# Moving two pairs of DMA transposes behind the x loads, and two spectrum loads two steps up, in a fused FFT-filter and mixer kernel

## The chip, the core and the metric

The kernel runs on one core of a Trainium2 chip. The time is the device time in microseconds (us) of one execution. The core has five engines that work side by side: PE (TensorE, matrix products), DVE (VectorE), ACT (ScalarE), POOL (GpSimd) and SP (SyncE). In this kernel DVE and ACT empty PE's result banks and do the elementwise work, SP issues most DMAs (transfers within the core's memory, between it and DRAM, and DMA transposes), and POOL issues the loads of x and the stores of the output. An engine works through its instructions in order: an instruction that waits holds back all that stand behind it on that engine.

## The reference

Two stages follow each other. The first is a global filter along the sequence, the second a low-rank mixing along the sequence with a two-layer channel network:

```python
batch, seq, dim = 8, 3136, 256          # rank 32, hidden 1024
X = np.fft.rfft(x, axis=1)
Y = X * (filt_r + 1j * filt_i)[None]
x = np.fft.irfft(Y, n=seq, axis=1)

h = x.transpose(0, 2, 1) @ U @ V        # mixes the sequence through rank 32
u = x + h.transpose(0, 2, 1)
out = u + np.maximum(u @ w_ch1, 0.0) @ w_ch2
```

Inputs and output are float32; the kernel computes in float16 with float32 sums.

## The kernel before, in words

The transform of length 3136 is split as 49 x 64. For each batch the kernel does these stages, in the code's names:

- `load_x`: four tiles of x per batch (called c = 0 to 3 here), issued by POOL, each 98 partitions by 2048 numbers, converted from float32 to float16 on the way. The tag has four buffers.
- `f1`: the 49-point transforms on PE (line 249), emptied by ACT (line 254). After every fourth step the result goes to DRAM (`ct1`, and `ct0` for the lowest frequency), issued by SP (lines 256 and 257). Sixteen steps per batch, four for each tile of x.
- `mid`: first the loads of `a2` from `ct1` and `ct0` (lines 327 and 330, SP). Then, for twelve pairs of frequencies and the lowest one, a product (`pz`, lines 384 and 386), the filter on DVE (line 392, then 396 and 397), and three steps later the way back (`pe`, line 344), which ACT copies to `e3` (line 354). Every second pair is written to DRAM by SP (line 362) in `ct2[b][0]`, `ct2[b][1]` or `ct2[b][2]`, two writes to each.
- `load_e2`: the three thirds of `ct2` come back as rows of `eb` (line 415), two DMAs of 256 KB for each third, issued by SP. `eb` has one buffer. The changed line names these thirds p = 0, 1, 2.
- `rank`: the low-rank part, on PE, ACT and DVE (DVE copies rows into `eb`, line 437).
- `s4`: the last transform (`pu`, line 455) from `eb` to `ut`, with the mixed sequence u in `ut`.
- The channel network runs over 49 groups of 512 rows of u. `mm1` (line 487) makes one eighth of the hidden layer, ACT applies the rectifier (line 490). `mm2` (line 520) makes the output of the group before. The summand u is added in one of two ways. For a group in `turning`, `turn_u` brings u turned into the tile `tur` by DMA transposes (line 500, two per piece of a batch, so one pair for most groups), issued by SP, and DVE adds it while it empties the bank (line 533). For the other groups PE adds it (line 512) and DVE only copies (line 536). `tur` has three buffers. POOL stores a group of the output (line 540).

The order is written out by hand. The main loop has 392 steps, eight per group: step 8n + t does `mm1` of group n and `mm2` of group n - 1 for part t, and then whatever `plan[8n + t]` holds. The loop `for b in range(1, NB)` fills the plan: while the channel network works on batch b - 1 (steps a to z, with a, z = `S[b-1]`, `S[b]`), the stages of batch b and the `f1` of batch b + 1 are dealt over the steps. `deal(gen, count, a, z)` puts `count` steps of a stage evenly between two steps. `e` marks the end of `mid`: e = 76, 124, 172, 220, 266, 314 for b = 2 to 7. For b = 2, a = 48 and z = 96.

The plan sets an order for each engine, not a time. An SP instruction runs as soon as those before it in SP's queue have been issued and what it reads, or the buffer it writes, is ready.

What stands in the plan around the change, for b = 2: `turn_u` of groups 7, 8 and 9 at steps 49, 50, 51; the four loads of x of batch 3 at steps 48 to 51; `ct2` writes at 53 and 57 (first third), 61 and 67 (second), 72 and 74 (last); `f1` of batch 3 from step 58 on, with its writes at 61, 65, 70 and 74; the loads of `eb` at 71, 72 and 77; the first step of `mid` of batch 3 (its `a2` loads) at 78; `s4` from step 85 on. For the later batches the same stands at the same distances from e, but for small shifts.

Of the kernel before, what the change touches and what calls it, by code (L numbers as in the profile page):

```python
# [79 lines left out]
def kernel(  # L80
# [465 lines left out]
    def deal(gen, count, a, z):  # L546
        for i in range(count):
            plan[max(0, int(a + i * (z - a) / count))].append(gen)

    def later_x(b, c):  # L550
        load_x(b, c)
        yield

    def turn_at(at, n):
        turning.add(n)
        plan[at].append(turns[n])
# [55 lines left out]
    def loads(b, part):  # L612
        load_e2(b, part)
        yield

    for b in range(1, NB):
        a, z = S[b - 1], S[b]
        e = z - (17 if b == 1 else 20 if b < 6 else 22)
        deal(mids[b], 13, a + {1: 8, 2: -3}.get(b, -5), e - 4)
        deal(mids[b], 4, e - 4, e)  # L620
        for p, at in enumerate((e - 5, e - 4, e + 1)):
            plan[at].append(loads(b, p))
        deal(ranks[b], 6, e, e + 6)
        if b + 1 < NB:

            plan[z - 12 if b == 1 else e + 2].append(mids[b + 1])

        n = a // 8 + (1 if b > 1 else 2)
        for i in range(3):
            turn_at(a + (15 if b == 1 else 1) + i, n + i)  # L630
        turn_at(z - (15 if b == 1 else 9), z // 8 - 1)
        deal(s4s[b], 16, e + (8 if b == 1 else 9), z - (2 if b == 1 else 1))
        if b == 1:
            deal(f1s[1], 12, 1, 8)
        if b + 1 < NB:

            for c in range(4):
                plan[a + {1: 9 + 2 * c, 2: c}.get(b, 2 * c - 8)].append(later_x(b + 1, c))
            deal(f1s[b + 1], 16, a + (21 if b == 1 else 10), z - (13 if b == 1 else 20))
# [43 lines left out]
```

## Time and profile before

| What | Value |
|---|---|
| median of the runs shown | 507.56 us (505.39 to 508.66) |
| time of the profiled execution | 509.21 us |
| its span (first to last recorded work) | 507.4 us |
| PE busy | 482.4 us (95%) |
| ACT busy | 375.7 us (74%) |
| DVE busy | 350.2 us (69%) |
| POOL busy | 82.4 us (16%) |
| mean granted PE clock | 0.996 of full speed |
| DMA | 97.26 MB, mean 192 GB/s |

The busy time of an engine is the time in which it works on an instruction; time in which it only waits is not in it. PE's busy time also holds time in which it runs at a lower clock. The time lies 1.8 us above the span: that part is outside the recorded work.

### The profile page before, as it was taken

The page shows a single profiled execution, that of the slowest core. Times are in us where ns is not written, and L with a number is a line of the kernel's source. Part 1 is how long each engine was busy: PE and PEld are TensorE (multiplying, and loading weights), DVE is VectorE, ACT ScalarE, POOL GpSimd, SP SyncE. Part 2 cuts the span into 40 slices and gives each one's busy share as a digit, 9 for nine tenths or more (in the row PEclk, how much of TensorE's full clock was granted, in tenths as well). Part 3 has the DMA queues.
Part 4 walks back from the last instruction along what each step waited for, and adds up shares of the span by engine and source line. Part 5 has one row for each costly group of instructions (what it writes and reads, how often), then busy time and mean ns, then how long its engine had stood idle before and what let it go on. Part 6 is the DMA issues. An engine that isn't in the chain of part 4 may idle for free.

```text
span 507.4 us, 11552 instructions
## 1 busy us (share of the span) xinstructions
PE 482.4 (95%) x4584; PEld 339.1 (67%) x4584; DVE 350.2 (69%) x470; ACT 375.7 (74%) x704; POOL 82.4 (16%) x125
## 2 busy tenths in 40 slices
PE   3788899997999999999999999999999999999997
PEld 3536566775667777677666777677667766776665
DVE  5796599588657897479747897579846995642122
ACT  6875778966796689857995689867996677666663
POOL 6773110012001200120102101021001010101110
PEclk9999999999899999999999999999999999999999
DMA  8998769989967995899678975899789447843343
GB/s 188 178 224 160 122 138 217 283 228 186 202 190 257 194 222 168 267 288 171 196 220 279 180 196 149 267 262 192 208 247 246 129 113 226 129 125 89 99 105 126
DMA packets 105383, 97.26 MB, mean 192 GB/s; under 512 B 42971, under 2 KB 89883, under 8 KB 105328
## 3 DMA queue, kind: packets, MB, share of 16 engines
q1 hardware_dynamic: 90560, 54.87, 46.4%
q0 software_dynamic: 14768, 41.65, 33.6%
q8 instruction: 36, 0.59, 0.5%
q14 instruction: 19, 0.16, 0.1%
HBM read 55.07 MB, written 47.64 MB: 202 GB/s over the span
## 4 chain that ended last, share of the span: by engine, by line
PE 75%; DMA 7%; DVE 5%; issue 4%; ACT 2%; POOL 1%; SPq 0%; POOLq 0%; ACTq 0%
PE pc L520 29%; PE phh L487 28%; PE pf L249 4%; PE pu L455 4%; PE pe L344 4%; PE pz L384 3%; DVE uv L392 3%; DMA x<-in_x_dram 3%; DMA w2sb<-in_moe_w_ch_dram 2%; DMA eb<-ct 2%; PE pc L512 1%; DMA ct<-e 1%; PE ph L422 1%; ACT e L354 1%; DVE uv L396 0%
## 5 line engine op out<-in xcount | busy, mean ns | idle before, releaser
L490 ACT ACTIVATE h<-phh 128x512 f16<-128x512 f32 x392 | 235.9, 604 | 80.7 <-PE phh L487 79.9
L520 PE MATMUL pc<-w2sb,h 128*128 128x256 f16 x1568 | 234.4, 273 | 1.3 <-DMA w2sb<-in_moe_w_ch_dram 0.8
L487 PE MATMUL phh<-ut,w1sb 128*128 128x512 f16 (+7 forms) x896 | 233.7, 353 | 0.5 <-DVE ut L462 0.5
L520 PEld LDWEIGHTS <-h 128*128 128x128 f16 x1568 | 151.9, 98 | 92.6 <-issue 2.4
L392 DVE TENSOR_TENSOR uv<-pz,fab 128x1024 f16<-128x1024 f32 (+1 forms) x104 | 120.4, 1178 | 11.1 <-PE pz L384 9.3
L540 POOL DMA_DIRECT2D out_dram<-och x48 | 38.8, 809 | 391.2 <-DVE och L533 256.8
L533 DVE TENSOR_TENSOR och<-pc,tur 128x512 f32<-128x512 f32 (+1 forms) x71 | 48.4, 682 | 76.7 <-PE pc L520 75.5
L487 PEld LDWEIGHTS <-w1sb 128*128 128x128 f16 x896 | 80.0, 97 | 20.6 <-issue 1.6
L354 ACT CAST e<-pe 128x512 f16<-128x512 f32 x96 | 56.6, 591 | 16.9 <-PE pe L344 16.0
L462 DVE CAST ut<-pu 128x392 f16<-128x392 f32 x92 | 48.3, 560 | 21.6 <-PE pu L455 18.5
L254 ACT CAST asb<-pf 98x512 f16<-98x512 f32 x96 | 57.3, 599 | 3.8 <-PE pf L249 3.5
L437 DVE COPY eb<-h 32x4096 f16<-32x4096 f16 x32 | 38.2, 1231 | 13.7 <-ACT h L434 13.7
L344 PE MATMUL pe<-uv,m 128*128 128x512 f16 (+1 forms) x117 | 41.5, 373 | 2.3 <-DVE uv L392 1.6
L455 PE MATMUL pu<-sv,eb 97*128 97x49 f16 x1024 | 39.1, 185 | 2.1 <-DMA eb<-ct 1.1
L249 PE MATMUL pf<-x,ws 98*98 98x256 f16 x192 | 37.0, 275 | 2.9 <-DMA x<-in_x_dram 2.8
L455 PEld LDWEIGHTS <-eb 97*128 97x128 f16 x1024 | 37.1, 96 | 3.9 <-issue 2.6
L384 PE MATMUL pz<-a,m 128*128 128x512 f16 x96 | 36.4, 381 | 1.1 <-DVE a L310 1.0
L396 DVE TENSOR_TENSOR uv<-uv 64x1024 f16<-64x1024 f16 (+1 forms) x49 | 30.8, 629 | 1.7
L249 PEld LDWEIGHTS <-ws 98*98 98x98 f16 x192 | 23.1, 127 | 12.8 <-issue 4.3
L397 DVE TENSOR_TENSOR uv<-uv 64x1024 f16<-64x1024 f16 (+1 forms) x49 | 30.8, 628 | 0.7
L536 DVE COPY och<-pc 128x512 f32<-128x512 f32 x28 | 19.4, 691 | 15.1 <-PE pc L512 13.8
L460 ACT CAST ut<-pu 128x392 f16<-128x392 f32 x36 | 17.5, 485 | 7.8 <-POOL seen L603 4.6
(80 smaller groups left out, 237.8 us busy)
## 6 DMA issues: line engine op xcount, KB each, us to landing
out_dram<-och POOLq DMA_DIRECT2D x48, 512.0 KB, 4.7
ct<-e SPq DMA_DIRECT2D x47, 256.0 KB
eb<-ct SPq DMA_DIRECT2D x46, 256.0 KB
x<-in_x_dram POOLq DMA_DIRECT2D x28, 392.0 KB, 10.0
ct<-asb SPq DMA_DIRECT2D x24, 384.0 KB
a<-ct SPq DMA_DIRECT2D x18, 512.0 KB
x<-in_x_dram POOLq DMA_DIRECT2D x4, 384.0 KB, 8.7
tur<-ut SPq DMA_TRANSPOSE x70
```

What stands on the lines that cost most here:

```text
L249: nc.tensor.matmul(pf[0:98, 256 * s:256 * s + 256], ws[:, (8 * c + j) * 98:(8 * c + j + 1) * 98], t[:, j, :], start=(s == 0), stop=True, s ...
L254: nc.scalar.copy(dst, src)
L344: nc.tensor.matmul(pe[:, 0:n], w, uv[:, f, o:o + n], start=(f == 0), stop=(b > 0 or f == 1))
L354: nc.scalar.copy(t[:, 2 * (i % 2):2 * (i % 2) + 2, :].rearrange("p k d -> p (k d)"), pe)
L384: nc.tensor.matmul(pz, a2m, src[:, k:k + 2, :].rearrange("p k d -> p (k d)"), start=True, stop=True)
L392: nc.vector.tensor_mul(uv[:, :, o:o + n], zin, fin)
L455: nc.tensor.matmul(pu[:, NQ * i:NQ * i + NQ], eb[:, 8 * n + i, d], sv[:, 8 * g + i, :], start=(i == 0), stop=True, skip_group_check=True)
L462: nc.vector.tensor_copy(dst, src)
L487: nc.tensor.matmul(ph[:, o:o + n], w1sb[:, dh, 128 * t:128 * t + 128], utv(b)[:, dh, t0:t0 + n], start=(dh == 0), stop=(dh == 1), skip_gro ...
L490: nc.scalar.activation(h, ph, RELU)
L520: nc.tensor.matmul(o, gr.h[tt][:, 128 * i:128 * i + 128], w2sb[:, tt, :], start=(tt == 0), stop=(tt == 7 and gr.n in turning), skip_group_ ...
L533: nc.vector.tensor_add(dst.rearrange("p g (h d) -> p g h d", h=2), src.rearrange("p (g h d) -> p g h d", h=2, d=128), gr.tu[:, :, a:a + n, ...
```

## The change

Two places of the loop that fills the plan are edited.

- The loads of `eb` of thirds 0 and 1 stand at steps e - 7 and e - 6 in place of e - 5 and e - 4, for every batch from b = 2 on. Third 2 stays at e + 1.
- For b = 2 alone, `turn_u` of groups 8 and 9 stands at steps 60 and 61 in place of 50 and 51. Group 7 stays at step 49.

No instruction is added or removed.

```diff
         e = z - (17 if b == 1 else 20 if b < 6 else 22)
         deal(mids[b], 13, a + {1: 8, 2: -3}.get(b, -5), e - 4)
         deal(mids[b], 4, e - 4, e)
-        for p, at in enumerate((e - 5, e - 4, e + 1)):
+        for p, at in enumerate((e - 5, e - 4, e + 1) if b == 1 else (e - 7, e - 6, e + 1)):
             plan[at].append(loads(b, p))
...
         n = a // 8 + (1 if b > 1 else 2)
         for i in range(3):
-            turn_at(a + (15 if b == 1 else 1) + i, n + i)
+            turn_at(a + {1: 15 + i, 2: (1, 12, 13)[i]}.get(b, 1 + i), n + i)
```

## The prediction

> **What bounds the kernel now.** I read the page first. PE is busy for nearly the whole span and carries 75% of the chain of work that ended last, so an edit that adds and removes no instruction can only change time in which PE waits, or PE's clock.
>
> ```profile
> PE 482.4 (95%) x4584; PEld 339.1 (67%) x4584; DVE 350.2 (69%) x470; ACT 375.7 (74%) x704; POOL 82.4 (16%) x125
> PE 75%; DMA 7%; DVE 5%; issue 4%; ACT 2%; POOL 1%; SPq 0%; POOLq 0%; ACTq 0%
> ```
>
> Next come the waits of PE, longest first. Asked stretch by stretch, those after the prologue that touch this change are two: the f1 of batch 3 waits for x, and the s4 of batch 4 waits for eb.
>
> ```profile
> PE pf L249 <- DMA x<-in_x_dram: 2.8, 1, 2.8
> PE pu L455 <- DMA eb<-ct: 1.1, 1, 1.1
> ```
>
> The chain in order of time (start, duration, what) shows where. The first wait ends at 127.09, the second at 273.80.
>
> ```profile
> 114.05 13.00 DMA x<-in_x_dram
> 127.05 0.04 issue
> 127.09 0.38 PE pf L249 x2
> ...
> 263.54 5.76 DMA ct<-e
> ...
> 269.35 4.31 DMA eb<-ct
> 273.66 0.14 issue
> 273.80 0.57 PE pu L455 x16
> ```
>
> The table by stretches shows that the first wait costs more than its length. Behind the busy times, the third column from the right is the granted clock: 0.58, 0.50, 0.50, 0.71 in the four microseconds after it.
>
> ```profile
> 128.00:129.00 1.00, 1.00 (x8) 0.69 (x6) 0.36 (x1) 0.60 (x2) 0.00 (x0) 0.58 1.27 214
> 129.00:130.00 1.00, 1.00 (x5) 0.53 (x4) 0.97 (x2) 0.51 (x2) 0.00 (x0) 0.50 1.34 134
> 130.00:131.00 1.00, 1.00 (x5) 0.48 (x4) 0.59 (x1) 0.73 (x3) 0.00 (x0) 0.50 1.19 102
> 131.00:132.00 1.00, 1.00 (x7) 0.79 (x6) 0.00 (x0) 0.53 (x2) 0.00 (x0) 0.71 1.88 87
> ```
>
> PE loses 0.42 + 0.50 + 0.50 + 0.29 = 1.71 us there. So the wait for x costs 2.82 + 1.71 = 4.53 us. After the wait for eb the clock stays at 1.00: that one costs 1.10 us.
>
> **Part 1, the transposes of groups 8 and 9.** SP's timeline has the six transposes of groups 7, 8 and 9 from 110.75 on, while POOL issues x from 114.05.
>
> ```profile
> 110.75 16.54 SPq L500 DMA_TRANSPOSE tur<-ut  x6
> 127.39 6.89 SPq L362 DMA_DIRECT2D ct<-e  x3
> ```
>
> Four transposes (groups 7 and 8) go at once. Group 9 needs the tur buffer of group 5, which DVE releases at 121.82 (an add at 121.14 for 0.68). All ct2 writes behind it stand until 127.39. The packet records say the same: a pair is 1,024 packets of 256 B; group 7's are through by 114, group 8's begin then and trickle at some 50 per us between 120 and 127, beside x packets of 322 ns.
>
> What does x take without them? The first x tile takes 13.0 us to land here and 12.7 in the next batch (issued at 164.80, transposes beside it). In the two batches after (220.80 and 278.29), where the records show the pairs in flight done before x starts, it is 6.5 and 6.1 us. So with group 8 away I expect the tile at 114.05 + 6.1 to 6.5 = 120.2 to 120.6, and PE asks for it at 127.09 - 2.82 = 124.27: a margin of 3.7 us. If nothing but half of the delay went, it would land at 123.8, still in time; the gain is bounded by 0 and 4.53 us, and I take 4.53, by the nearest rows.
>
> The Trainium skill, page "DMA: Bandwidth & Descriptors", section "Queues, rings and completion order", speaks against this: each DMA engine takes turns between its rings, a packet at a time. By that, 31 ns of transpose beside each 322 ns x packet would slow x by a tenth, and x would have been in time already. The 13.0 against 6.1 us does not agree. It is rival B's ground.
>
> What the moved pairs meet: in SP's queue they now stand behind the ct2 writes of steps 53 and 57. The second of those waits for ACT's copy at 123.44 + 0.58 = 124.02, so group 8's pair goes at some 124.5, group 9's after the next ct2 write. They need 1.2 to 2.5 us of SP each. Behind them are ct2 and ct1 writes, which today leave at 127.39 to 134.41 anyway. DVE wants the turned rows at steps 75 and 83, over 15 us later. The second to fourth x tiles, by the rows of 220.80 (8.1, 9.7, 11.8 us), land by 122.7 to 127.6; PE needs them four, eight and twelve steps after 124.27, a step being some 1.3 us, so from 129 on. What is late next is DVE: it lags PE by 1.5 us at 124.4 (a product of 122.90 read at 124.40). The same lag stands at 184.10 in the next batch, where PE waits for nothing. So I put nothing there.
>
> **Part 2, the loads of two thirds of eb.** SP's timeline in batch 3:
>
> ```profile
> 197.53 0.39 SPq L362 DMA_DIRECT2D ct<-e  x1
> 201.61 0.30 SPq L256 DMA_DIRECT2D ct<-asb  x1
> 201.96 0.39 SPq L257 DMA_DIRECT2D ct<-asb  x1
> 202.40 1.23 SPq L415 DMA_DIRECT2D eb<-ct  x2
> 203.73 0.54 SPq L362 DMA_DIRECT2D ct<-e  x1
> 204.37 2.24 SPq L415 DMA_DIRECT2D eb<-ct  x2
> 206.66 0.65 SPq L362 DMA_DIRECT2D ct<-e  x1
> ```
>
> Two steps up, the first third goes right behind the ct2 write of 197.53, the second as soon as that write has landed; both now stand ahead of the ct1 write of 201.61. This adds a wait at the head of SP's queue. The packets of that write end at 199.5, and the DMA engines then idle:
>
> ```profile
> 199.50:201.50 2.00, 2.00 (x16) 1.43 (x15) 1.95 (x3) 1.97 (x5) 0.00 (x0) 1.00 0.00 0
> ```
>
> So both thirds fit into time in which neither SP nor the DMA engines do anything (256 to 258 and 313 to 315.5 read 0.00 as well). Should the write land as late as the slowest one on the chain (5.76 us), the second third would leave at some 203.7, still before today's 204.37; the ct1 and first ct2 writes would slip by 2 us, the last ct2 write, held by ACT, by nothing.
>
> What it is worth: in batch 4 the last ct2 write leaves at 263.54, though ACT was done at 262.14 + 0.63 = 262.77, because SP was issuing loads (260.75 for 2.74). It then shares the DMA engines with them for 5.76 us. After the change it leaves 0.77 us sooner and shares less. If it lands no faster for that, 0.3 us of the wait stay; if it lands like the one of 197.53 (about 2 us), the last load starts at 265 and the margin is over 3 us. I take the whole 1.10 us; bounds 0 and 1.10. PE starts s4 of the other batches without a wait, so there the loads earn nothing.
>
> **The sum.** 2.82 + 1.71 + 1.10 = 5.63 us. The profiled execution (509.21: span 507.4 and 1.8 around it) would become 503.6. It is 1.65 us above the median of the runs shown, about the price of the slow clock. From the median the sum gives **501.9 us**, a ratio of 0.989. I forecast against the median: 502.0.
>
> **The rivals.**
>
> A. The stall goes, but the slow clock was not in the runs of the median: 1.65 us, the profiled run's excess, is close to 1.71. Then the gain is 2.82 + 1.10 = 3.92: 503.6 us. The Trainium skill, page "TensorE: Matmul & The Clock Gate", section "Part 1: The HAM clock gate (the "warmup" mystery)", has the clock fall after an idle window of about 3.4 us that runs free, so a gap of 2.82 would not surely cost it. The trace has it fall after 2.82. Chance 0.18.
>
> B. x is late for another reason: in both slow cases the output store issued just before (113.31 and 164.06) is beside it. For: POOL's queue serves both. Against: a store precedes x at 220.05 and 277.55 too, with 6.5 and 6.1 us. Then only part 2 counts: 507.56 - 1.10 = 506.5. Chance 0.10.
>
> C. Slower: the moved pair meets the second x tile instead of the first. It decides if that tile is still in flight at 124.5, that is, if it takes over 9.9 us from its issue at 114.61. Its delay would be the one seen, 13.0 - 6.3 = 6.7 us, so it would land near 129.2 to 131, and the third and fourth could each stall PE too. One such stall with its clock merely replaces today's 4.53; two cost 4.53 more, less 1.10: 511.0. For it: the ct2 write of step 53 now runs beside x at 119.4. Against: 8.1 and 7.7 us in the undisturbed rows. Chance 0.08.
>
> D. The plan moves but the issue does not: an SP instruction runs when its data allow, and loads that wait for a write could leave when they do now. Against: SP is idle at 199 to 201, and group 8 has been ready at 110.75. 507.6 us. Chance 0.04.
>
> **How the numbers follow.** The forecast has 0.60. Its own range is 500.0 to 503.6, the spread of the runs shown (2.2 us below the median) and the price of the clock. For 8 in 10, I go from 500.0 up through A to near B: **499.9 to 506.0**, which leaves out C, D and most of B (about 0.2). About 1% is what a measurement of this kernel can tell from no change; that is 502.5, just above the forecast. Of the forecast's 0.60, 0.52 lie below 502.5, and of A's 0.18, 0.03. So faster 0.55, slower 0.07 (C and a little for what I don't see), within 1% 0.38.
>
> **What would show it.** Right: no wait for x at line 249 in the profile, first x tile of batch 3 landing within 7 us, granted clock 1.00 around 128; SP showing two transposes at 110.75 and the other four behind two ct2 writes near 124 to 132; loads of eb at some 198 to 201 in batch 3, less 4.5; no wait at line 455 in batch 4. Wrong: a wait for x that moved to the second tile, a first tile still at 13 us, or a new wait of PE for eb, because SP stood at the head of its queue for a ct2 write.

## The result and the profile after

The changed kernel takes 502.85 us in the median (501.83 to 503.59), the kernel before 506.92 (505.39 to 508.66) beside it. The ratio is 0.9917, with a 95% interval of 0.9893 to 0.994. Timed again later it is 502.23 against 507.38 us, ratio 0.9900 (0.9873 to 0.9927). So it is faster by 0.8 to 1.0%; the forecast was 502.0 us and 0.989. Executions that lie over 1.5% above the fastest of the same kernel are left out of the ratios and of the counts below, which concerns five of the kernel before.

The profiled execution shortened more: 501.83 us with a span of 500.1, against 509.21 and 507.4. These are the same views of the page as before, engines' busy time and shares of the chain:

```profile
PE 481.2 (96%) x4584; PEld 339.1 (68%) x4584; DVE 350.2 (70%) x470; ACT 375.7 (75%) x704; POOL 82.5 (17%) x125
PE 85%; DMA 6%; DVE 4%; ACT 2%; POOL 1%; issue 1%; SPq 0%; POOLq 0%; ACTq 0%
```

PE's share of the chain went from 75 to 85%, that of issue from 4 to 1%: between 110 and 135 us the chain now stays on PE, where before it came from a store and an x load. Of PE's waits between 58 and 470 us, one is left in the changed kernel, and it stood in the kernel before too:

```profile
PE pz L384 <- DVE a L310: 1.0, 2, 0.7
```

**Where the time went.** Each group's store (line 540) marks the same point of the work in both kernels, so the difference of their issue times shows where time was saved. Two windows of POOL's timeline, the stores of groups 4 to 6 with the four x loads between them; before, then after:

```profile
113.31 0.75 POOL L540 DMA_DIRECT2D out_dram<-och  x1 [9.74 <-DVE och L533]
114.05 2.18 POOL L127 DMA_DIRECT2D x<-in_x_dram  x4
122.11 0.79 POOL L540 DMA_DIRECT2D out_dram<-och  x1 [5.89 <-DVE och L533]
136.76 0.77 POOL L540 DMA_DIRECT2D out_dram<-och  x1 [13.86 <-DVE och L536]
```

```profile
111.91 0.75 POOL L540 DMA_DIRECT2D out_dram<-och  x1 [9.74 <-DVE och L533]
112.65 2.19 POOL L127 DMA_DIRECT2D x<-in_x_dram  x4
120.72 0.79 POOL L540 DMA_DIRECT2D out_dram<-och  x1 [5.88 <-DVE och L533]
130.71 0.78 POOL L540 DMA_DIRECT2D out_dram<-och  x1 [9.20 <-DVE och L536]
```

| store of group | before minus after, us |
|---|---|
| 0 to 5 | 1.39 to 1.40 |
| 6 to 20 | 6.05 to 6.06 |
| 21 to 47 | 7.30 to 7.31 |

The first 1.40 us were saved ahead of everything that the change touches (the prologue varies so from one execution to the next). The change gives 4.65 us at the f1 of batch 3 and 1.26 us at the s4 of batch 4, and nothing else moves by 0.1 us: **5.91 us in the trace, against a forecast sum of 5.63.** The tables below read every profile in this way, from the store of group 4 on.

SP's timeline shows the moved pairs. The first two transposes go at 109.36, the ct2 writes of steps 53 and 57 no longer stand behind the others, and the moved pairs follow them:

```profile
109.36 2.52 SPq L500 DMA_TRANSPOSE tur<-ut  x2
118.07 4.95 SPq L362 DMA_DIRECT2D ct<-e  x2
123.12 4.32 SPq L500 DMA_TRANSPOSE tur<-ut  x2
127.88 0.37 SPq L362 DMA_DIRECT2D ct<-e  x1
128.34 2.67 SPq L500 DMA_TRANSPOSE tur<-ut  x2
```

The first x tile of batch 3 lands 6.0 us after its issue in place of 13.0. The line of its load, asked for alone, and two stretches of the table, in which the granted clock (third column from the right) stays full where it was 0.50:

```profile
DMA to landing us min/median/max: 6.0/6.0/6.0
```

```profile
126.00:128.00 2.00, 2.00 (x17) 1.38 (x15) 1.25 (x2) 1.83 (x5) 0.00 (x0) 1.00 1.21 318
128.00:130.00 2.00, 2.00 (x18) 1.56 (x17) 1.92 (x4) 1.93 (x5) 0.00 (x0) 1.00 1.35 110
```

The moved loads of eb in batch 3 go right behind the ct2 write, all four in one go:

```profile
191.48 0.39 SPq L362 DMA_DIRECT2D ct<-e  x1
191.92 3.11 SPq L415 DMA_DIRECT2D eb<-ct  x4
195.56 0.31 SPq L256 DMA_DIRECT2D ct<-asb  x1
195.91 0.39 SPq L257 DMA_DIRECT2D ct<-asb  x1
197.58 3.30 SPq L362 DMA_DIRECT2D ct<-e  x2
201.00 0.45 SPq L256 DMA_DIRECT2D ct<-asb  x1
201.49 0.46 SPq L257 DMA_DIRECT2D ct<-asb  x1
203.11 1.16 SPq L415 DMA_DIRECT2D eb<-ct  x2
```

SP has issued them all by 195.03, before ACT has the next ct1 write ready (195.56). In between SP waits 0.7 us for the ct2 write to land (0.3 us in batch 4), and no wait of PE comes of it. SP's own waits from 191 to 196 us have this line:

```profile
SPq L415 <- DMA ct<-e: 0.7, 1, 0.7
```

The load of the last third leaves at 203.11; before, it was 211.86, which is 205.81 less the 6.05 us that the trace is ahead here. So it is 2.7 us sooner. In batch 4 it goes from 269.35 to 259.34, 3.96 us sooner by the same reckoning, and PE's wait of 1.10 us is gone. The last third in batch 3 before, then in batch 4 after:

```profile
211.86 1.83 SPq L415 DMA_DIRECT2D eb<-ct  x2
```

```profile
259.34 1.16 SPq L415 DMA_DIRECT2D eb<-ct  x2
```

### The profile page after: what moved, and what is told of

The parts are those of the page before. It is cut to its first block, busy times and chain, and to the rows that moved or that the text cites. A ratio compares the mean times of both kernels' runs of the same rounds, so it can differ in the third digit from the quotient of the medians.

```text
span 500.1 us, 11540 instructions
## 1 busy us (share of the span) xinstructions
PE 481.2 (96%) x4584; PEld 339.1 (68%) x4584; DVE 350.2 (70%) x470; ACT 375.7 (75%) x704; POOL 82.5 (17%) x125
## 4 chain that ended last, share of the span: by engine, by line
PE 85%; DMA 6%; DVE 4%; ACT 2%; POOL 1%; issue 1%; SPq 0%; POOLq 0%; ACTq 0%
PE pc L520 33%; PE phh L487 32%; PE pu L455 5%; PE pf L249 4%; PE pe L344 4%; PE pz L384 4%; DVE uv L392 2%; DMA w2sb<-in_moe_w_ch_dram 2%; DMA x<-in_x_dram 2%; PE ph L422 1%; PE pc L512 1%; DMA fab<-in_filt_i_dram 1%; DMA eb<-ct 1%; POOL x L127 1%; ACT a L310 1%
## 5 line engine op out<-in xcount | busy, mean ns | idle before, releaser
L437 DVE COPY eb<-h 32x4096 f16<-32x4096 f16 x32 | 38.2, 1231 | 13.7 <-ACT h L434 13.7
```

## The experiments

### One part at a time

Each part alone, on one chip with the kernel before:

```diff
-            turn_at(a + (15 if b == 1 else 1) + i, n + i)
+            turn_at(a + {1: 15 + i, 2: (1, 12, 13)[i]}.get(b, 1 + i), n + i)
```

> Only the two pairs of transposes move; the loads stay. My theory (transposes beside x make its first tile late; the wait costs 2.8 us and 1.7 us of half clock): the wait for x at line 249 is gone, the first tile of batch 3 lands in 6 to 7 us, the store of group 6 is issued 4.5 to 4.7 us sooner behind that of group 5 than before, the wait of 1.1 us for eb in batch 4 stays; about 4.5 us below the kernel before in a profile, 3 to 4.5 us in the medians. Rival (the clock was lost in the profiled run alone): 2.8 us or less in the medians. Rival (x is late beside the store): no gain.

```diff
-        for p, at in enumerate((e - 5, e - 4, e + 1)):
+        for p, at in enumerate((e - 5, e - 4, e + 1) if b == 1 else (e - 7, e - 6, e + 1)):
```

> Only the loads of the first two thirds of eb move; the transposes stay. My theory: the wait for x and the half clock stay, the wait for eb in batch 4 goes, worth 1.1 to 1.3 us from there on and nothing elsewhere: 1.1 us below the kernel before, or 0.2%. Rival (the loads at the head of SP's queue hold back the last third): PE waits for eb at the start of an s4, the same or slower.

The kernel before was also run under a name of its own, without an edit.

> The kernel before, unchanged, to see how its two waits vary from one execution to the next. My theory, that the waits belong to the order of the instructions: the profile has a wait for x of 2 to 3.5 us with some 3.4 us of half clock behind it, and the mean clock of the runs is near 0.996 to 0.998 in all of them. Rival (the half clock falls on a window that runs free, so that a gap of 2.8 us is met by it only sometimes): a part of the runs has a mean clock as high as the changed kernel's (0.998 to 1.000) and is 1.5 to 2 us shorter.

| kernel | median us (ratio, interval) | store 6, against before | store 21, against before |
|---|---|---|---|
| transposes alone | 503.76 (0.994, 0.9912 to 0.9969) | -4.65 | -4.49 |
| loads alone | 507.51 (1.0001, 0.9972 to 1.0031) | -0.57 | -1.83 |
| before, again | 507.54 (0.9994, 0.997 to 1.0019) | +0.41 | +0.40 |
| whole change | 502.85 (0.9917, 0.9893 to 0.994) | -4.65 | -5.91 |

A minus sign is sooner. The kernel before had 507.38 us in the median beside the first three; the last row is the first comparison again. The parts keep to their places. With the transposes alone, the wait for x is gone and that for eb stays; with the loads alone it is the other way round. PE's waits, first of the transposes alone (200 to 300 us), then of the loads alone (60 to 300 us):

```profile
PE pu L455 <- DMA eb<-ct: 1.3, 1, 1.3
```

```profile
PE pf L249 <- DMA x<-in_x_dram: 2.3, 1, 2.3
PE pz L384 <- DVE a L310: 1.0, 2, 0.7
```

From store 20 to store 21 the loads alone gain 1.83 - 0.57 = 1.26 us, as in the whole change. The 0.57 us before that are a shorter wait for x, 2.3 in place of 2.8 us; the unchanged kernel shows 3.6 us in the other profile taken of it, so that wait varies by over a microsecond. In the medians of this comparison the loads show nothing. So the transposes alone and the whole change were timed again side by side.

> The changed kernel as it is, timed on the same chip as the next one, so that the share of the loads shows in the medians. My theory: 4 to 4.5 us below the kernel before (executions of the kernel before with full clock are 2.8 us above it), mean clock 0.998 to 1.000 in nearly all executions.

> The two pairs of transposes moved and the loads of eb left, beside the whole change on the same chip. My theory: the wait of 1.1 to 1.3 us for eb in batch 4 is in most executions, so the median is 0.8 to 1.3 us above that of the whole change. Rival (the loads bring nothing outside single executions): within 0.4 us of the whole change.

The whole change took 502.23 us, the transposes alone 503.69 (ratio 0.9934, 0.9914 to 0.9954): the medians differ by 1.46 us once the larger wait is gone. That is near the 1.26 us of the profile, a little above the range expected, but the executions (6 and 12) overlap, and drawing them anew at random many times puts the difference at 0.4 to 2.4 us in 95% of the draws. The profile of the transposes alone has the eb wait again, 1.0 us.

That wait is not in every execution. Of the eight profiles in this document with the loads in their old places, six have it in batch 4 and two do not (the kernels with work in the wait and with x sooner, both below). None of the five with the loads moved has it.

### The clock by itself

The prediction priced the slow clock at 1.71 us. To measure it without touching a DMA, PE was given work in the wait:

```diff
                     pf = bank("z", "pf")
+                    if b == 3 and c + half + i == 0:
+                        unread(pf, 12)
```

> The kernel before, with twelve products that nobody reads (128x512, 0.216 us each, 2.6 us together) put on PE ahead of the first f1 product of batch 3, where PE waits for x. They measure the clock by itself: x lands when it did, but PE is not idle meanwhile. My theory: the wait for x shrinks to 0.2 to 0.5 us, the clock stays at 1.00 behind it, and from there on the profile is some 1.7 us sooner than before. Rival (the slow clock is not a consequence of the idle time, but falls there anyway): half clock near 128 stays, nothing gained. Where a run's wait for x is shorter than 2.6 us, the twelve products cost the difference.

Line numbers of this kernel are two higher. PE's timeline has the twelve products, and the first f1 product right behind them; the table of stretches has the clock at full speed:

```profile
122.83 2.75 PE L265 MATMUL pf<-m 128*128 128x512 f16 x12
125.66 0.38 PE L251 MATMUL pf<-x,ws 98*98 98x256 f16 x2
```

```profile
125.00:127.00 2.00, 1.92 (x14) 1.20 (x13) 0.00 (x0) 0.92 (x2) 0.00 (x0) 1.00 1.10 219
127.00:129.00 2.00, 2.00 (x15) 1.33 (x13) 1.91 (x2) 1.68 (x5) 0.00 (x0) 1.00 1.22 159
```

The store of group 6 is 1.82 us sooner than in the profile of before, which is the price of the half clock to 0.1 us, as far as one execution can tell (the x tile lands a microsecond sooner or later from one to the next). From the store of group 9 on the gain is 1.55 us. The 2.80 us at store 21 hold also the eb wait, which is missing in this execution. The median is 505.98 us (ratio 0.9975, 0.9949 to 1.0002), and all twelve executions have a mean clock of 0.999 or 1.000. So it is the idle PE time that turned the clock down: no DMA was touched, and work that nobody reads holds it up.

How often does it fall? Every timed execution has its span and mean clock. One half-speed stretch of 3.41 us (the length in the first profile) takes 0.5 x 3.41 / 507 = 0.0034 off the mean, two take 0.0067. Over 78 executions of the kernel before, from the comparisons in "The experiments":

| mean clock | executions | median us |
|---|---|---|
| 0.999 and over (no stretch) | 36 | 505.73 |
| 0.995 to 0.998 (one) | 36 | 507.84 |
| under 0.995 (two) | 6 | 509.0 |

Nearly half have none. With the five executions that are left out, the lower two rows would hold 39 and 8. The number of stretches is inferred from the mean, which does not say where they fall: three of the 36 in the middle row read 0.998, and the profiled execution of the changed kernel reads that for a stretch at its end, from 498.4 us on. With the transposes alone, where no wait for x is left, 4 of 24 executions still read 0.995 to 0.997. The profiled execution that the prediction was worked out from had one. The rival stated for the unchanged kernel, that the gap meets the window only sometimes, holds: in its 12 executions under a name of its own, 4 have a mean clock of 0.999 or 1.000.

The Trainium skill, page "TensorE: Matmul & The Clock Gate", section "Part 1: The HAM clock gate (the "warmup" mystery)", describes a free-running window of about 3.4 us and two states of the clock, half and full. The stretches here measure 3.413 us and twice that (6.83), at 0.50, which agrees. Gaps of 2.3, 2.8, 3.3 and 3.6 us, below and above a window, each cost one stretch in the profiles, and one of 3.0 us cost two, so a gap need not be as long as the window.

### Which pair, and what x waits for

```diff
-            turn_at(a + (15 if b == 1 else 1) + i, n + i)
+            turn_at(a + {1: 15 + i, 2: (1, 12, 3)[i]}.get(b, 1 + i), n + i)
```

> The kernel before with the transposes of group 8 alone moved behind the ct2 writes (step 60); group 9's stay at step 51, where they wait for their buffer until DVE has added group 5, which is some 8 us after x is issued. My theory (it is the pair in flight when x starts that holds its first tile): no wait for x at the first f1 product, first tile within 7 us of its issue, store of group 6 about 4.6 us sooner against that of group 5, as with both moved. Rival (group 9's pair, which runs from 122 on beside the later tiles, is what counts): the wait stays, or moves to a later tile.

The other one has `(1, 2, 13)[i]` in this place.

> The kernel before with the transposes of group 9 alone moved (step 61); group 8's stay at step 50 and go beside x. My theory: the wait for x of 2.3 to 3.6 us stays, with the half clock behind it, and the first tile takes 12 to 14 us to land; nothing gained. Rival: no wait, 4.6 us gained.

Both kept the wait, 3.0 and 3.3 us, with the first tile landing after 13.2 and 13.5 us; nothing was gained (one execution of each, 510.19 and 512.04 us; the second also has two waits for eb, 2.2 us together). The first was a miss of mine, and SP's timeline of it says why:

```profile
110.27 5.96 SPq L500 DMA_TRANSPOSE tur<-ut  x4
118.99 4.95 SPq L362 DMA_DIRECT2D ct<-e  x2
124.03 5.27 SPq L500 DMA_TRANSPOSE tur<-ut  x2
```

Four transposes go at once, not two. The buffers of `tur` are handed out in the order of the calls: with group 8 called later, group 9 took the buffer that was already free and went straight away. So both kernels have a second pair issued beside x (at 112.85 and 114.16 us with x at 113.57 in the first), whichever group's it is, and in both x is late; which pair it is was not told apart. In the first the wait of 3.0 us was followed by two half-speed stretches, seen in the table of stretches as 0.50 and below full until near 133, which is why its store 6 is 1.49 us later than before's:

```profile
128.00:130.00 2.00, 2.00 (x10) 1.23 (x9) 0.65 (x1) 0.61 (x2) 0.00 (x0) 0.50 1.31 318
130.00:132.00 2.00, 2.00 (x9) 1.20 (x8) 1.26 (x2) 1.54 (x3) 0.00 (x0) 0.50 0.82 117
132.00:134.00 2.00, 2.00 (x14) 1.39 (x13) 0.00 (x0) 1.32 (x3) 0.00 (x0) 0.77 0.00 0
```

Next, the pairs half as far, right behind the first ct2 write and in the middle of the x loads:

```diff
-            turn_at(a + {1: 15 + i, 2: (1, 12, 13)[i]}.get(b, 1 + i), n + i)
+            turn_at(a + {1: 15 + i, 2: (1, 6, 7)[i]}.get(b, 1 + i), n + i)
```

> The changed kernel with the transposes of groups 8 and 9 at steps 54 and 55 in place of 60 and 61: behind one ct2 write, so that group 8's pair goes some 6 us after x is issued and not 11 (near 118.5 where the first tile lands at 118.7). My theory: the first tile lands in 6 to 7 us and PE doesn't wait for it; the pair now holds the second and third tile, which land some 4 to 6 us later than the 7 and 10 us of the changed kernel, near 125 to 128, where PE needs them at 128 and 133: no wait, or under 1 us; the time of the changed kernel within 0.3%. Rival (a pair beside any part of x costs a stall as before): a wait of 2 to 4 us at the second tile, with half clock.

```profile
117.53 0.37 SPq L362 DMA_DIRECT2D ct<-e  x1
117.94 10.08 SPq L500 DMA_TRANSPOSE tur<-ut  x4
```

No wait for x: 501.93 us (ratio 0.9898, 0.9873 to 0.9924), beside 502.23 for the change itself on the same chip, and store 21 at -5.90. But the second half of my expectation failed, to the good: the second to fourth tiles land after 7.7, 10.5 and 12.6 us, as in the changed kernel (7.6, 10.5, 12.9). A pair issued in the middle of the x loads did not hold up those that were already queued. A second pair issued at the same time as x made the first tile late in each of the six profiles that have one (12.5, 12.8, 13.0, 13.2, 13.5 and 13.7 us). In the six where both pairs go later it took 6.0 to 7.0 us.

The same edit for the next batch, whose first x tile had taken 12.7 us:

```diff
-            turn_at(a + {1: 15 + i, 2: (1, 12, 13)[i]}.get(b, 1 + i), n + i)
+            turn_at(a + {1: 15 + i, 2: (1, 12, 13)[i], 3: (1, 12, 13)[i]}.get(b, 1 + i), n + i)
```

> The changed kernel with the same two pairs ten steps later in the stretch of batch 3 as well (groups 14 and 15), where the first x tile took 12.7 us in the kernel before and PE did not wait. My theory: that tile lands in 6 to 7 us, and the time is that of the changed kernel, within 0.3%, since no wait stood there. Rival (x in that batch is late for another reason than the transposes): 12 us stay.

The time is that of the change, 502.54 us (ratio 0.994, 0.991 to 0.997) and store 21 at -5.91. The tile takes 8.2 us, not 6 to 7; but it takes 8.3 in the changed kernel too, and 7.1 in the second profile of the kernel before. The 12.7 us did not come again, so this experiment says nothing on the cause. It does not speak against the transposes either: in the execution with 12.7 us SP issued the second one of a pair 1.53 us ahead of x, and in the 12 other profiles that was 2.17 us or more ahead at this place, with 7.1 to 8.6 us.

### The other way to separate them: x first

```diff
-                plan[a + {1: 9 + 2 * c, 2: c}.get(b, 2 * c - 8)].append(later_x(b + 1, c))
+                plan[a + {1: 9 + 2 * c}.get(b, 2 * c - 8)].append(later_x(b + 1, c))
```

> The kernel before with the four loads of x of batch 3 at steps 40, 42, 44 and 46 in place of 48 to 51, so that POOL issues them behind the store of group 3 instead of group 4, some 10 us sooner and ahead of all transposes of the stretch; transposes and loads of eb stay. My theory (only the first tile's lateness matters, not the order of the transposes): the wait for x goes, the same 4.6 us are gained up to group 6, and the wait for eb in batch 4 stays. Rival (x now meets the loads of eb or a2, or the transposes of groups 7 and 8 wait behind x and DVE for their rows): a new wait, less gained.

This is slower, 509.42 us (ratio 1.0064, 1.0026 to 1.0101). The wait for x is gone (and in this execution that for eb, which was expected to stay), but x, issued from 102.92 to 105.10, now meets the `a2` loads of batch 2, issued at 106.04:

```profile
PE pz L384 <- DMA a<-ct: 5.7, 1, 5.7
```

```profile
106.04 9.32 DMA a<-ct
115.36 0.05 issue
115.41 0.61 PE pz L384
```

A wait of 5.7 us, with half clock (0.50) from 114 to past 120, takes the place of 2.8 us. That the `a2` loads are late because of x is argued from these times. That x must move behind something, not ahead, is shown for this stretch only.

## Why the prediction was right

- **The wait for x and the transposes.** Right, and by the step given: first tile in 6.0 us where 6.1 to 6.5 were read from the undisturbed batches, the wait gone, 4.65 us where 4.53 were summed. Two of the rows behind it were weaker than they read. The 12.7 us of the next batch did not come again. And in the undisturbed batch of 220.80 the packets of the pair run from 221 to 223 us, so they are done before the packets of x but not before its issue; there the pair was issued at 216.37 and 217.72, over 3 us ahead of x.
- **The slow clock.** This is the term that was mis-sized. The forecast took 1.71 us from the median as if every execution paid it. By the clock table 36 of 78 pay nothing and 6 pay twice, which makes (36 x 1.71 + 6 x 3.42) / 78 = 1.05 us on average, an estimate that puts every stretch down to this wait. The sum is then 2.82 + 1.05 + 1.10 = 4.97 us, between the 4.07 and 5.15 us of the two pairs of medians. The rival that stated this (A, 503.6 us) was as near to the 502.85 of the first comparison as the forecast was; to the 502.23 of the second the forecast is nearer. The truth lies between the two.
- **The loads.** Right in place, 1.26 us against 1.10 in the profile. The wait that this adds at the head of SP's queue came, 0.7 us, and harmed nothing: the loads are issued from 191.92 to 195.03, in time in which SP had nothing to issue. The 1.10 us were taken as if every execution paid them; two of eight profiles do not.
- **What the moved pairs meet, and DVE's lag.** Right: no wait at a later tile, and none at line 384 for DVE that was not there before.
- **The rivals.** B (the store beside x) is out: the same store is issued 0.74 us ahead of x in the changed kernel, which lands in 6.0 us. C (the second tile) is out: 7.6 us. D (the issue does not move) is out by SP's timeline.
- **The size.** Faster by over 1% had a chance of 0.55. The first comparison gives 0.83%, the second 1.0%, and the intervals span that line.

## What to carry to other kernels

Price a short wait of PE by the clock as well as by its length, but as a chance: read the mean clock of all executions, not the one that was profiled. Where a load is late though its queue is free, look for what was issued on the other queue at that time; putting that behind the load can be worth more than starting the load sooner, which here ran into the next transfer. And moving a call changes which buffer it gets, and so whether it waits.

## What was not expected of the hardware

A second pair of DMA transposes, issued on SP's queue as POOL issues x (at 113.3 and 114.6 us beside 114.05 in the first profile), doubled the time of the first x tile (12.5 to 13.7 us against 6.0 to 7.0). The same pair issued 6 us into the loads cost them nothing (12.6 us for the last tile, against 12.9 and 11.9 in the two profiles of the changed kernel). The Trainium skill, page "DMA: Bandwidth & Descriptors", section "Queues, rings and completion order", has each engine take turns between its rings by packets; the second case agrees with that, the first does not follow from it.

What holds x in the first case was not tried further and stays open, but the traces narrow it. A load counts as landed at the sixteenth of its semaphore updates. In the six late profiles fourteen of the sixteen are in 6.5 to 7.8 us after the issue, close to the 5.8 to 6.4 of the six with the pairs moved, and only the last two come at 11.0 to 13.7 us. So most of the tile's updates are on time, and two hold PE. Being issued close together is not enough to bring this about: the last x tile of batch 2 goes alone at 72.53 us, 0.06 us behind a transpose, and takes 7.5 us (7.1 to 7.7 over the 13 profiles).
